# Loads cast on GpSimd's queue and transposed tile by tile, and score bursts that run across batches, in a fused attention and MLP kernel

## The chip, the cores and the metric

The kernel runs on one core of a Trainium2 chip. The metric is the device time of one execution in microseconds (us); less is better. The engines are named as in the profile: PE (TensorE matmul), PEld (its weight loads), DVE (VectorE), ACT (ScalarE), POOL (GpSimd), SP (SyncE, here only a queue that issues DMAs).

## The reference

Attention with causal mask over 8 batches and 8 heads, 576 queries, and 16 extra "beacon" keys and values that every query sees, then an MLP with a squared ReLU over the 4608 resulting tokens:

```python
k_all = np.concatenate([beacon_k, k], axis=2)      # (8, 8, 16 + 576, 64)
v_all = np.concatenate([beacon_v, v], axis=2)
scores = scale * np.matmul(q, k_all.transpose(0, 1, 3, 2))
# causal mask on the 576 keys, softmax over all 592
x = np.matmul(a, v_all)  # then laid out as (4608, 512)
h = x @ w_in             # (512, 2048)
out = (np.maximum(h, 0.0) ** 2) @ w_out            # (2048, 512)
```

Inputs and output are float32; the kernel computes in bf16 and accumulates in float32.

## The kernel before, in words

Work is cut by batch. A batch has four pairs of heads; a pair's two heads use the upper and the lower 64 rows of PE at the same time ("rows" mode). Keys come in five tiles of 128 rows (the last has 80), of which the first holds the 16 beacons.

Per batch: Q and K are brought into the transposed layout (`qT`, `kT`, head dimension on the partitions). Score matmuls (L813) write scores, transposed, into PSUM, ACT takes the exponential into `pt` (L830), DVE applies the causal mask (L848, L852), PE multiplies with V and a column of ones (AV, L869), DVE normalises into `xn` (L884, L885), and `xn` is transposed into `xT`, a ring of four batches, by SP's DMA transposes (L916; batch 0 on PE, L933). The MLP runs over nine chunks of 512 tokens: first product L997, ReLU on ACT or DVE (L1014, L1016), square on DVE (L1023), second product L1037, evacuation on ACT and a store on SP (L1062). The last chunk ends with L1080.

Score pieces. The scores of a pair are cut into four pieces with 512, 512, 512 and 128 columns for each head (`WHOLE`). A piece fills a pair of PSUM banks. PE does them in bursts, since rows mode and the full mode of the other matmuls alternate. From batch 1 on the fourth pieces of two pairs share one pair of banks (`SHARED`), with an exponential for each: 14 pieces a batch. `SIZES` gives the bursts: from batch 2 on 3, 3, 3, 3 and 2 pieces, so a batch's last burst has two.

Q, K and V. Batches 0 to 2 load Q and K strided (L635, POOL's queue, which casts to bf16 while loading; the first pair by SP and ACT, cast by copies) and transpose them on PE (L671, L674). V of batches 0 and 1 is loaded by POOL's queue with the cast in the DMA (L498, L499; `SOFT_V`). Everything else, that is V of batches 2 to 7 and Q and K of batches 3 to 7, is loaded by SP in float32 into eight staging tiles `stg` (L512, L513) and cast by POOL (L452) into `vb` or into the Q and K areas in `qk_area`. When all five tiles of Q, or of K, have been cast, one DMA transpose on SP turns 20 blocks of 128 x 128 (L543). Q and K areas, V and `qT`, `kT` are double-buffered by batch; the last Q and K tile are zeroed by POOL once (L476, L477).

Order. `Order` is a list scheduler that runs while the kernel is built: each piece of work (`Op`) has an engine, a cost, a priority, dependencies and perhaps a claim on a pool (PSUM banks, staging tiles, `pt` slots). It plays the costs forward, with a model of the DMA rings, and emits the instructions in the order that comes out. On the chip each engine follows its order and waits on semaphores. `gate` in `add_pair` holds back the scores of a pair until the MLP has come far enough. `TURNS` (L315) fixes by hand the order in which POOL issues the first loads. While PE has nothing to do near the start, `filler` emits small matmuls on an identity matrix (L571, L569; L559 first), in the window `FILL` (0.6 to 22 us of the scheduler's time); `OWED` is the number of fillers that are put in after each operation named in `ahead` whether PE has other work or not, and is 0. SP and POOL work strictly in order: an issue that waits holds all behind it.

Of the kernel before, what the change touches and what calls it, by code (L numbers as in the profile page):

```python
# [130 lines left out]
class Order:  # L131
# [5 lines left out]
    FILL = (0.6, 22.0)  # L137
    OWED = 0
# [20 lines left out]
    def run(self):  # L159
# [25 lines left out]
        now = 0.0  # L185
        mode = None
        owed = 0
        while events:
# [27 lines left out]
            while again:  # L216
                again = False
                for e in engines:
# [33 lines left out]
                    if e == "PE" and self.filler is not None and self.FILL[0] <= now < self.FILL[1] and (  # L252
                            best is None or owed):
# [50 lines left out]
        for op, e, _ in issued:  # L304
# [10 lines left out]
TURNS = ("tri0 sld0k1 sld0q1 sld0k2 sld0q2 sld0k3 sld0q3 ld0v0 ld0v1 win0 ld0v2 tri1 ld0v3 ld0v4 win1 win2 win3 bkl1 sld1k0 sld1q0 sld1k2 sld1q2 ld1v0 ld1v1 ld1v2 ld1v3 ld1v4 "  # L315
         "wout0 wout1 wout2 bkl2 sld2k0 sld2q0 wout3 sld2k2 sld2q2")
# [3 lines left out]
def kernel(  # L320
# [29 lines left out]
    def sb(name, shape, dt):  # L350
        return pool.tile(shape, dt, name=name)

    NSTG, NPT, RB = 8, 4, 4
# [9 lines left out]
    qb = [qk_area[:, (2 * i) * W:(2 * i + 1) * W].rearrange("p (g c d) -> p g c d", g=HP, c=NT)  # L363
          for i in range(2)]
    kb = [qk_area[:, (2 * i + 1) * W:(2 * i + 2) * W].rearrange("p (g c d) -> p g c d", g=HP, c=NT)
# [4 lines left out]
          for i in range(2)]  # L370
    bks = sb("bks", [128, H, D], BF16)
# [29 lines left out]
    def wait_for(later, first):  # L401
# [4 lines left out]
        pools={"ps": Banks(), "stg": Slots(NSTG), "pt": Slots(NPT)},  # L406
# [63 lines left out]
    SOFT_V = [(b, c) for b in range(2) for c in range(NT)]  # L470
# [3 lines left out]
    def add_zero(b):  # L474
        def emit(e):
            nc.gpsimd.memset(qb[b % 2][:, :, NT - 1, :], 0.0)  # L476
            nc.gpsimd.memset(kb[b % 2][:, :, NT - 1, :], 0.0)  # L477
        deps = trans[NPE - 1, "q"] + trans[NPE - 1, "k"] + trans[NPE - 2, "q"] + trans[NPE - 2, "k"]
        zero_ops[b] = add(f"zero{b}", "POOL", 1.0, emit, prio=10.0 * b - 1, deps=deps)

    def add_load(b, x, c, prio, behind=[], sync=[]):
# [6 lines left out]

        soft = (b, c) in SOFT_V
        queue = nc.gpsimd if soft else nc.sync  # L490

        if soft:

            def emit_soft(e):
                to = vb[b % 2][:, c, :, 0:D]
                insts = []
                if lo:
                    insts.append(queue.dma_start(out=to[0:Nb], in_=beacon[b].transpose([1, 0, 2])))  # L498
                insts.append(queue.dma_start(out=to[lo:rows], in_=t[b, :, t0:t0 + rows - lo, :].transpose([1, 0, 2])))  # L499
                return insts  # L500

            ld = add(f"ld{b}{x}{c}", "POOL", 1.3 if lo else 0.65, emit_soft, prio=prio, dma=0.85 * rows / 128 + 0.1 * (lo > 0), packet=0.0135,
                     behind=load_chain[-1:] + behind, sync=sync)
            load_chain.append(ld)
            cast[b, x, c] = ld
            return

        def emit_load(e):
            st = stg[ld.held[0]]
            insts = []  # L510
            if lo:
                insts.append(queue.dma_start(out=st[0:Nb], in_=beacon[b].transpose([1, 0, 2])))  # L512
            insts.append(queue.dma_start(out=st[lo:rows],  # L513
                                         in_=t[b, :, t0:t0 + rows - lo, :].transpose([1, 0, 2])))
            return insts

        ld = add(f"ld{b}{x}{c}", "SP", 1.3 if lo else 0.65, emit_load,
                 prio=prio, take=("stg", "stg", [1]), dma=1.2 * max(rows / 128, 0.72) + 0.2 * (lo > 0), behind=load_chain[-1:] + behind, sync=sync)
        load_chain.append(ld)

        def emit_cast(e):
            st = stg[ld.held[0]]
            if x == "v":
                copy_on(e, vb[b % 2][0:rows, c, :, 0:D], st[0:rows])
            else:
                dst = (qb if x == "q" else kb)[b % 2][0:rows, :, c, :]
                copy_on(e, dst, st[0:rows].rearrange("p (g u) d -> p g (u d)", u=2))

        deps = [ld]
# [7 lines left out]
        cast[b, x, c] = add(f"cast{b}{x}{c}", "POOL", 0.65, emit_cast, prio=prio, deps=deps, give=ld)  # L537

    def add_trans(b, x, prio):
        srcb, dst = (qb, qT) if x == "q" else (kb, kT)  # L540

        def emit(e):
            nc.sync.dma_start(  # L543
                out=dst[b % 2].rearrange("p g (c t) -> p (g c) t", c=NT),
                in_=srcb[b % 2].rearrange("p g c d -> p (g c d)"),
                transpose=True,
            )

        deps = [cast[b, x, c] for c in range(NT)]
        deps += [o for p in range(HP * (b - 2), HP * (b - 1)) for o in qk_ops[p]]  # L550
        trans[b, x] = [add(f"tr{b}{x}", "SP", 3.8, emit, prio=prio, deps=deps, dma=3.4, margin=2.0)]

    def filler(spot, mode, now):
# [19 lines left out]
        op = Op("fill", "PE", 0.11, emit, mode=mode)  # L573
# [180 lines left out]
    PIECES = {b: ONE_BY_ONE if b < 1 else SHARED for b in range(B)}  # L754
    SIZES = {b: [2] * 7 if b < 2 else [3, 3, 3, 3, 2] for b in range(B)}
# [29 lines left out]
    def add_scores(pairs, n, sizes, pieces):  # L785
# [10 lines left out]
        for size in sizes:  # L796
            group = work[at:at + size]
            at += size
            lead = group[0][0][0]
            prio = 100.0 * lead.p + 1000.0 * n + group[0][0][1]  # L800
            every = [part for parts in group for part in parts]
            cols = sum(t1 - t0 for _, _, _, (mms, _, _) in every for _, t0, t1, _ in mms)
            owners = list({x.p: x for x, _, _, _ in every}.values())
            box = {}

            def emit_qk(e, group=group, box=box):
                for k, parts in enumerate(group):
                    st = pair(box["qk"], k)
                    for x, _, lo, (mms, _, _) in parts:
                        for c, t0, t1, col in mms:  # L810
                            for hj in range(2):
                                hp = slice(64 * hj, 64 * hj + 64)
                                nc.tensor.matmul(  # L813
                                    st[:, hj, lo + col:lo + col + t1 - t0],
                                    kT[x.b % 2][hp, x.pr, 128 * c:128 * c + 128],
                                    qT[x.b % 2][hp, x.pr, t0:t1],
                                    start=True, stop=True,
                                )

            qk = add(f"qk{lead.p}.{n}.{group[0][0][1]}", "PE", cols / 2400.0, emit_qk, prio=prio,  # L820
                     deps=[d for x in owners for d in x.qk_deps + [x.take_pt] + early.get((x.b, x.pr, min(n, 1)), [])],
# [373 lines left out]
```

## Time and profile before

| what | value |
|---|---|
| median of 3 runs | 337.18 us (337.08 to 338.04) |
| the profiled execution | 337.61 us |
| its span | 335.7 us |
| granted PE clock, mean | 1.00 |
| DMA engines, 0 to 220 us | mean busy share mostly 0.8 and above |
| HBM read, written | 37.22 MB, 9.44 MB |

The span runs from the first to the last recorded instruction; the profiled execution's time is 1.9 us more. Times inside the trace are counted from the span's start. In rows of instructions the fields are line, engine, operation, what is written <- what is read, count, then busy time, mean duration in ns of one, and the idle time of the engine ahead of them with what ended it. In the chain in order of time a row has its start, its duration, and engine, tile, line and count. A few per cent of the matmul records are missing, so counts can be a little short.

### The profile page before, as it was taken

The numbers are of one execution on the slowest core, as the hardware profiler recorded it, in microseconds if no ns is written. First come the engines' busy times: TensorE is split into PE (matmuls) and PEld (weight loads), VectorE is DVE, ScalarE is ACT, GpSimd is POOL, SyncE is SP. The second block draws the span as 40 slices with busy tenths as digits, with TensorE's granted clock in tenths as the row PEclk, the third lists the DMA queues.
The fourth block names the chain that finished last, engine by engine and source line by source line (L and its number), as shares of the span: only waits on it lengthen the run. The fifth ranks groups of instructions, "written<-read, shape, count | busy, mean of one in ns | idle before, by whom it ended". The sixth has DMA issues, their size and how long they took to land.

```text
span 335.7 us, 7764 instructions
## 1 busy us (share of the span) xinstructions
PE 326.6 (97%) x3190; PEld 184.3 (55%) x3231; DVE 159.9 (48%) x329; ACT 194.1 (58%) x296; POOL 84.2 (25%) x130
## 2 busy tenths in 40 slices
PE   7899999999999999999999999999999999999996
PEld 5568765554555455545468945554545444444444
DVE  6689985557423762376136812681258303301400
ACT  3887977577465647574566555665576226515611
POOL 8946504513224332223242240420000000000000
PEclk9999999999999999999999999999999999999999
DMA  8999999899979996899799898973110321011003
GB/s 139 173 204 186 200 205 211 143 235 189 226 113 254 236 213 137 204 232 201 133 253 219 180 182 176 209 155 70 64 64 0 63 71 62 2 62 62 2 5 120
DMA packets 144180, 49.17 MB, mean 146 GB/s; under 512 B 130577, under 2 KB 139665, under 8 KB 144145
## 3 DMA queue, kind: packets, MB, share of 16 engines
q1 hardware_dynamic: 125168, 39.63, 58.2%
q0 software_dynamic: 18624, 8.69, 20.1%
q8 instruction: 25, 0.41, 0.5%
q10 hardware_dynamic: 352, 0.36, 0.4%
q14 instruction: 11, 0.08, 0.1%
HBM read 37.22 MB, written 9.44 MB: 139 GB/s over the span
## 4 chain that ended last, share of the span: by engine, by line
PE 91%; POOL 3%; DMA 3%; issue 1%; DVE 1%; ACT 0%; DVEq 0%
PE ps L997 37%; PE ps L1037 36%; PE ps L869 8%; PE ps L813 8%; DMA w_in<-in_moe_w_in_dram 3%; POOL vb L499 1%; PE ps L671 1%; POOL qk_area L635 1%; PE ps L1080 1%; POOL tri L435 0%; DVE g L1016 0%; POOL w_in L958 0%; DVE tri L414 0%; PE ps L933 0%; POOL vb L498 0%
## 5 line engine op out<-in xcount | busy, mean ns | idle before, releaser
L997 PE MATMUL ps<-xT,w_in 128*128 128x512 bf16 (+3 forms) x688 | 133.7, 340 | 1.2 <-DVE g L1016 0.2
L1037 PE MATMUL ps<-w_out,g 128*128 128x512 bf16 x535 | 125.1, 379 | 1.8 <-issue 0.6
L830 ACT ACTIVATE pt<-ps 128x1024 bf16<-128x1024 f32 (+3 forms) x128 | 103.1, 870 | 28.9 <-PE ps L813 27.8
L997 PEld LDWEIGHTS <-w_in 128*128 128x128 bf16 x704 | 65.5, 98 | 55.5 <-issue 4.1
L1014 ACT ACTIVATE g<-ps 128x512 bf16<-128x512 f32 (+2 forms) x111 | 63.3, 570 | 44.1 <-PE ps L997 43.9
L1037 PEld LDWEIGHTS <-g 128*128 128x128 bf16 x560 | 52.2, 98 | 61.7 <-issue 4.0
L1023 DVE TENSOR_TENSOR g<-g 128x1024 bf16<-128x1024 bf16 (+2 forms) x80 | 51.4, 648 | 65.3 <-ACT g L1014 64.8
L450 ACT COPY osb<-ps 128x512 f32<-128x512 f32 (+2 forms) x37 | 21.3, 576 | 56.7 <-PE ps L1037 43.4
L452 POOL CAST qk_area<-stg 128x512 bf16<-128x512 f32 (+2 forms) x50 | 32.7, 659 | 66.1 <-DMA stg<-in_k_dram 33.2
L848 DVE TENSOR_TENSOR pt<-pt,tri 128x1024 bf16<-128x1024 bf16 (+1 forms) x36 | 23.6, 656 | 40.7 <-ACT pt L830 40.7
L869 PEld LDWEIGHTS <-pt 128*128 128x128 bf16 (+1 forms) x960 | 33.7, 97 | 6.6 <-issue 0.6
L452 POOL CAST vb<-stg 128x512 bf16<-128x512 f32 (+1 forms) x30 | 21.9, 734 | 58.9 <-DMA stg<-in_v_dram 52.9
L1016 DVE TENSOR_SCALAR g<-ps 128x512 bf16<-128x512 f32 (+2 forms) x49 | 28.9, 590 | 15.6 <-PE ps L997 15.3
L869 PE MATMUL ps<-vb,pt 128*128 128x65 bf16 (+1 forms) x960 | 35.0, 193 | 0.3 <-DMA vb<-in_v_dram 0.3
L813 PE MATMUL ps<-qT,kT 64*128 64x80 bf16 (+6 forms) x680 | 32.1, 230 | 0.0
L885 DVE TENSOR_TENSOR xn<-ps,rcp 128x640 bf16<-128x640 f32 (+2 forms) x36 | 27.0, 751 | 1.4
L813 PEld LDWEIGHTS <-kT 64*128 64x128 bf16 x680 | 18.2, 95 | 16.3 <-issue 13.5
L884 DVE RECIPROCAL rcp<-ps 128x10 f32<-128x10 f32 (+2 forms) x36 | 7.6, 211 | 32.6 <-PE ps L869 31.5
L450 ACT COPY qT<-ps 128x576 bf16<-128x576 bf16 (+2 forms) x13 | 7.7, 601 | 4.6 <-PE ps L671 3.3
L452 DVE COPY kT<-ps 128x576 bf16<-128x576 bf16 (+2 forms) x13 | 9.0, 706 | 2.6 <-PE ps L671 2.0
L852 DVE TENSOR_TENSOR pt<-pt,tri 80x160 bf16<-80x160 bf16 x32 | 9.8, 308 | 0.0
L499 POOL DMA_DIRECT2D vb<-in_v_dram x10 | 8.5, 851 | 3.5 <-DMA w_in<-in_moe_w_in_dram 3.1
(54 smaller groups left out, 80.8 us busy)
## 6 DMA issues: line engine op xcount, KB each, us to landing
out_dram<-osb SPq DMA_DIRECT2D x17, 512.0 KB, 3.4
stg<-in_q_dram SPq DMA_DIRECT2D x20, 256.0 KB, 4.8
stg<-in_v_dram SPq DMA_DIRECT2D x18, 256.0 KB, 4.7
stg<-in_k_dram SPq DMA_DIRECT2D x15, 256.0 KB, 4.8
w_in<-in_moe_w_in_dram POOLq DMA_DIRECT2D x4, 512.0 KB, 9.6
w_out<-in_moe_w_out_dram POOLq DMA_DIRECT2D x4, 512.0 KB, 9.8
stg<-in_v_dram SPq DMA_DIRECT2D x6, 224.0 KB, 4.5
qk_area<-in_k_dram POOLq DMA_DIRECT2D x4, 288.0 KB, 12.0
```

The source lines that it names most:

```text
L450: nc.scalar.copy(dst, src)
L452: eng[e].tensor_copy(dst, src)
L813: nc.tensor.matmul(st[:, hj, lo + col:lo + col + t1 - t0], kT[x.b % 2][hp, x.pr, 128 * c:128 * c + 128], qT[x.b % 2][hp, x.pr, t0:t1], sta ...
L830: nc.scalar.activation(pt[x.take_pt.held[0]][:, :, off:off + width], pair(box["qk"], k)[:, :, lo:lo + width], AF.Exp, bias=0.0, scale=scale)
L848: nc.vector.tensor_tensor(out=d, in0=d, in1=tri[:, m0:m0 + m, :][:, None].to_broadcast([128, 2, m, 128]), op=ALU.min)
L869: nc.tensor.matmul(a[:, hj, (t - tl[0]) * (D + 1):(t - tl[0] + 1) * (D + 1)], P[0:rr, hj, o:o + 128], vb[b % 2][0:rr, c, h, 0:D + 1], star ...
L885: nc.vector.tensor_tensor(out=xn[b % 2].rearrange("p t (h d) -> p h t d", d=D)[:, 2 * pr:2 * pr + 2, tl[0]:tl[0] + nt], in0=a[:, :, :, 0:D ...
L997: nc.tensor.matmul(h[:, lo - spans[0][0]:hi - spans[0][0]], w_in_sb[:, mc, ft * 128:(ft + 1) * 128], xT[:, mc, lo % RING:lo % RING + hi - lo],
L1014: nc.scalar.activation(dst, h, AF.Relu, bias=0.0, scale=1.0)
L1016: nc.vector.tensor_scalar(out=dst, in0=h, scalar1=0.0, scalar2=None, op0=ALU.max)
L1023: nc.vector.tensor_tensor(out=d, in0=d, in1=d, op=ALU.mult)
L1037: nc.tensor.matmul(o, G[:, fc, ts * 128:(ts + 1) * 128], w_out_sb[:, fc, :], start=(fc == 0), stop=(fc == NFT - 1))
```

## The change

1. **Loads.** All tiles of V, and Q and K of batches 3 to 7, are loaded on POOL's queue with the cast in the DMA, straight into `vb` and the Q and K areas. Staging is only kept for one small tile; POOL's casts are gone. The areas are laid out tile by tile. The first load of each of batches 4 to 7 waits for the transposes of K tile 3 of the batch before.
2. **Transposes.** Q and K of batches 3 to 7 are transposed one tile (four blocks) at a time on SP, 10 DMAs a batch in place of 2. A tile's K blocks of the four pairs go to `kT` side by side; a function `keys_of` that names this order is new, while the score matmuls address `kT` by pair and tile, as before.
3. **Pieces.** In batches 3 to 7 (`FLOW = 3`) the fourth pieces of all four pairs form one piece with one exponential into a tile `rest` (in the free tail of `qk_area`), from which AV reads these keys. A batch has 13 pieces. They go into bursts of three that are filled across the batch boundary: a batch's pieces left over start a burst with the first pieces of the next.
4. **Start.** `tri0` (two mask tiles on POOL) comes behind the six strided loads, not ahead of them. No filler between 5.0 and 6.2 us of the scheduler's time; the scheduler counts 0.13 for a filler (0.11 before), and `OWED` is 1. V of batch 2 follows its Q and K in the order fixed by hand.

In the instruction streams: SP has 107 instructions (160 before), of them 50 transposes of Q and K (10 before) and none of the 91 staging loads; POOL has 91 load issues more and 80 casts less; PE has the same matmuls for scores, AV and MLP, in 49 stretches of score matmuls (52 before), and 60 filler matmuls on the identity (76 before); ACT has 15 exponentials less.

```diff
-    FILL = (0.6, 22.0)
-    OWED = 0
+    FILL = ((0.6, 5.0), (6.2, 22.0))
+    OWED = 1
...
-TURNS = ("tri0 sld0k1 sld0q1 sld0k2 sld0q2 sld0k3 sld0q3 ld0v0 ...
+TURNS = ("sld0k1 sld0q1 sld0k2 sld0q2 sld0k3 sld0q3 tri0 ld0v0 ...
...
-    NSTG, NPT, RB = 8, 4, 4
+    NSTG, NPT, RB = 1, 4, 4
...
+    rest = [qk_area[:, 4 * W + 1024 * i:4 * W + 1024 * (i + 1)].rearrange("p (h w) -> p h w", h=2) for i in range(2)]
...
+        def emit_load(e):
+            if x == "v":
+                to = vb[b % 2][:, c, :, 0:D]
+            else:
+                to = (qb if x == "q" else kb)[b % 2][:, c].rearrange("p g (u d) -> p (g u) d", u=2)
+            insts = []
+            if lo:
+                insts.append(nc.gpsimd.dma_start(out=to[0:lo], in_=beacon[b].transpose([1, 0, 2])))
+            insts.append(nc.gpsimd.dma_start(out=to[lo:rows], in_=t[b, :, t0:t0 + rows - lo, :].transpose([1, 0, 2])))
+            return insts
...
+        for c in range(NT):
+            def emit(e, c=c):
+                if x == "q":
+                    to = qT[b % 2][:, :, 128 * c:128 * c + 128]
+                else:
+                    to = kT[b % 2].rearrange("p g t -> p (g t)")[:, 128 * HP * c:128 * HP * (c + 1)].rearrange(
+                        "p (g t) -> p g t", g=HP)
+                return [nc.sync.dma_start(out=to, in_=(qb if x == "q" else kb)[b % 2][:, c].rearrange("p g d -> p (g d)"),
+                                          transpose=True)]
...
-            if b == 2 and n == 0:
-                sync = [w_ops["out", 3]]
+            if b > NPE and n == 0:
+                sync = [trans[b - 1, "k"][3]]
...
+    def add_flow(pairs, last):
...
+        pieces = WHOLE[0].pieces
+        (c, t0, t1, _), = pieces[3][0]
+        flow.append([(x, 3, 128 * n, ([(c, t0, t1, 0)], None, 128)) for n, x in enumerate(pairs)])
+        flow.extend([(x, i, 0, pieces[i])] for x in pairs for i in range(3))
+        done = []
+        while len(flow) >= 3 or (last and flow):
+            group = [flow.pop(0) for _ in range(min(3, len(flow)))]
+            add_burst(group, 0, flow_exps)
...
+                        if x is not None and (c, t) == (0, 3):
+                            keys = rest[x.take_rest.held[0]][:, hj, 128 * pr:128 * pr + 128]
```

More of the change, by code (lines that the diff above doesn't have):

```diff
@@ L405 @@
     order = Order(
[L406 removed]
+        pools={"ps": Banks(), "stg": Slots(NSTG), "pt": Slots(NPT), "rest": Slots(2)},
         limits={"late": 4, "strip": 6, "av": 4, "mlp": 4, "tp": 6},
@@ L487, in add_load @@
             t0, rows = t_start(c), rows_of(c)
[L489 to L529, printed above, removed]
+        deps = []
         if x == "v" and b >= 2:
@@ L796, in add_scores @@
         for size in sizes:
-            group = work[at:at + size]
+            add_burst(work[at:at + size], n, exps)
             at += size
[L799 to L818, printed above, removed]
```

156 lines of the change are left out of this document (103 added, 53 removed).

## The prediction

> **What bounds the kernel now.** I read three views first: busy time by engine with the chain that ended last (the page), then busy time in stretches of 10 us, then the waits of PE.
>
> ```profile
> PE 326.6 (97%) x3190; PEld 184.3 (55%) x3231; DVE 159.9 (48%) x329; ACT 194.1 (58%) x296; POOL 84.2 (25%) x130
> ...
> PE 91%; POOL 3%; DMA 3%; issue 1%; DVE 1%; ACT 0%; DVEq 0%
> ```
>
> ```profile
> 0.00:10.00 10.00, 7.67 (x115) 5.18 (x115) 6.38 (x28) 4.29 (x6) 8.52 (x18) 1.00 0.90 146
> 10.00:20.00 10.00, 9.40 (x170) 6.51 (x164) 7.03 (x24) 8.05 (x13) 8.07 (x14) 1.00 1.70 182
> 20.00:30.00 10.00, 9.86 (x156) 7.80 (x153) 9.25 (x28) 7.79 (x13) 4.63 (x6) 1.00 1.29 203
> 30.00:40.00 10.00, 9.93 (x143) 7.92 (x141) 9.26 (x24) 9.47 (x20) 6.60 (x10) 1.00 1.71 186
> ```
>
> ```profile
> PE ps L1037 <- issue: 0.6, 4, 0.2
> PE ps L997 <- DVE g L1016: 0.2, 1, 0.2
> ```
>
> The columns of the stretches are PE, PEld, DVE, ACT, POOL, granted clock, DMA share, GB/s. From 20 us on PE is busy 9.86 and more of ten; the two wait rows (total, times, longest) are all that PE waited from 24 us to the end, 0.8 us. So the loads, casts, transposes and exponentials of batches 3 to 7 are hidden today: making them cheaper is worth nothing by itself, and making them late costs one for one. Only two things can shorten the run: fewer microseconds of matmul stream, and less lost time before 20 us. Granted clock is 1.00 in each of these rows.
>
> **Part 1: bursts of score matmuls (batches 3 to 7).** The cost of entering and leaving a burst is read from the chain in order of time, at a place with nothing missing around it.
>
> ```profile
> 231.60 0.77 PE ps L813 x20
> 232.38 4.21 PE ps L1037 x19
> 236.63 1.03 PE ps L1037 x4
> 237.66 0.67 PE ps L813 x20
> 238.33 1.83 PE ps L1037 x8
> 240.16 0.91 PE ps L869 x30
> 241.13 1.67 PE ps L1037 x7
> ...
> 263.45 1.08 PE ps L1037 x5
> ...
> 277.26 8.85 PE ps L997 x41
> ```
>
> By the code 64 matmuls of 512 columns run from 263.45 to 277.26 (a few records are missing): 13.81 / 64 = 0.216 us each. The eight at 238.33 should take 1.73 and took 1.83: leaving a burst costs 0.10 us. After AV matmuls (240.16) the next eight take from 241.07 to 242.80, 1.73: those switches are free. Inside a burst two heads run side by side. The one at 237.66 streams 1280 columns by the code, 1280 x 0.216 / 512 = 0.54, and took 0.67; the one at 231.60 streams 1536, 0.65, and took 0.77. Entering costs 0.13. So one burst costs 0.23 us beyond its columns.
>
> Before, a batch has 14 pieces in bursts of 3, 3, 3, 3, 2: 5 x 5 = 25 bursts. After, a batch has 13 pieces (four fourth pieces in one) and the 65 pieces run on: 22 bursts. Columns, AV matmuls and MLP matmuls stay as many as they were. The term is 3 x 0.23 = **-0.7 us**. ACT loses 15 small exponentials, which nothing waits for.
>
> **Part 2: the start.** What stands first on POOL, PE and the DMA engines:
>
> ```profile
> 1.68 0.53 POOL L435 TENSOR_SCALAR_AFFINE_SELECT tri<-tri 128x128 bf16<-128x128 bf16 x2 [1.16 <-DVE tri L414]
> 2.17 0.76 POOL L635 DMA_DIRECT2D qk_area<-in_k_dram  x1
> ...
> 6.84 1.73 POOL L499 DMA_DIRECT2D vb<-in_v_dram  x2
> ```
>
> ```profile
> 4.89 2.03 PE L571 MATMUL ps<-ident 128*128 128x128 bf16 x30
> 6.76 0.42 PE L671 MATMUL ps<-ident,sparek 96*128 96x96 bf16 x6
> ...
> 9.66 0.45 PE L674 MATMUL ps<-ident,qk_area 96*64 96x96 bf16 x12 [0.39 <-DMA qk_area<-in_q_dram]
> ...
> 13.57 0.46 PE L869 MATMUL ps<-vb,pt 128*128 128x65 bf16 x10 [0.33 <-DMA vb<-in_v_dram]
> ...
> 17.55 0.57 PE L997 MATMUL ps<-xT,w_in 128*128 128x240 bf16 x4
> ```
>
> ```profile
> 5.19 0.83 ACT L450 CAST spareq<-g 96x768 bf16<-96x768 f32 x1 [2.43 <-DMA g<-in_q_dram]
> ```
>
> ```profile
> 2.00:3.00 1.00, 1.00 (x3) 0.36 (x4) 0.81 (x8) 0.76 (x2) 1.00 (x3) 1.00 0.79 169
> 3.00:4.00 1.00, 1.00 (x3) 0.30 (x2) 1.00 (x8) 0.00 (x0) 0.99 (x3) 1.00 1.08 354
> ```
>
> tri0 stands in front of POOL's first load and waits for VectorE until 1.68; it ends at about 2.2. With tri0 behind the six loads, the first of them can go 1.2 us earlier (2.17 against some 1.0), and all that follows tri0 (V, W_in) by the wait alone, about 0.65 us. The 30 fillers end at 6.9 although the second operand of the first transpose was cast by 6.02: with 12 of them PE is free at 5.7, so the first transpose can go about 0.65 us earlier. In all the stream has 16 fillers less, 16 x 2.03 / 30 = 1.1 us.
>
> Bounds of this term: at best -1.2 us, everything moved up by what POOL gains. At worst it is +0.3 us: the DMA engines already have a share of 0.79 and 1.08 from 2 to 4 us, so POOL's earlier loads only share them with the first K and Q, whose casts then come later; the waits at 9.66 and 13.57 then stay where they are, fillers turn into waiting, and the bit more work that VectorE has before the first MLP matmul (a Q evacuation moves to it) costs a few tenths. I take the middle of the rows that speak for it, **-0.6 us** (the 0.65 that both the fillers and the V and W_in loads give), since PE has 0.39 + 0.33 us of waits and those fillers to lose before 17.55 and hardly anything afterwards.
>
> The second new thing, one owed filler after each of 16 named operations, is inside the count of 16 fewer.
>
> The Trainium skill (TensorE: Matmul & The Clock Gate, What's actually happening) says that PE falls to half its clock after an idle window of some 3.4 us. The gap without fillers, 5.0 to 6.2, is shorter, so by that page too it costs nothing; no run here shows it yet.
>
> **Part 3: loads and transposes, hidden if they are in time.**
>
> ```profile
> L452 POOL CAST qk_area<-stg 128x512 bf16<-128x512 f32 (+2 forms) x50 | 32.7, 659 | 66.1 <-DMA stg<-in_k_dram 33.2
> L452 POOL CAST vb<-stg 128x512 bf16<-128x512 f32 (+1 forms) x30 | 21.9, 734 | 58.9 <-DMA stg<-in_v_dram 52.9
> L499 POOL DMA_DIRECT2D vb<-in_v_dram x10 | 8.5, 851 | 3.5 <-DMA w_in<-in_moe_w_in_dram 3.1
> ...
> xT<-xn SPq DMA_TRANSPOSE x35, 2.5
> ```
>
> ```profile
> 90.92 8.40 SPq L916 DMA_TRANSPOSE xT<-xn  x5
> ...
> 127.30 6.91 SPq L916 DMA_TRANSPOSE xT<-xn  x5
> ...
> 147.03 0.53 SPq L1062 DMA_DIRECT2D out_dram<-osb  x1
> ```
>
> ```profile
> 116.97 0.54 PE ps L813 x8
> ...
> 137.51 0.86 PE ps L997 x4
> ```
>
> POOL loses 80 casts (54.6 us) and gains 91 load issues of at most 0.85 us (77 us), spread over some 170 us: it stays under half busy, but now the first load of each of batches 4 to 7 waits for K transposes of the batch before (a new wait), and behind it on POOL stand all later loads. SP loses 91 issues and has 50 transposes of four blocks, which I price by xT, the same shape: 1.4 to 1.7 us each on SP (6.91 / 5, 8.40 / 5), 2.5 to landing.
>
> The tightest place is batch 4, since the burst with the last piece of batch 3 now also holds the first two of batch 4 and needs all its transposes. In the new order as much PE work stands ahead of this burst as was done in the old run about 1 us after the burst at 116.97, so it wants them at about 117 (with 1 us gained by then). On SP they stand behind the five xT transposes of batch 2, which begin no later than at 90.92: 90.9 + 5 x 1.4 + eight transposes x 1.4 + two stores x 0.53 + 2.5 = 112.7; at 1.7 each it is 116.6. Slack 0.4 to 4 us. XT of batch 3 now stands behind five Q transposes of batch 5; begun at the old 127.30, its third tile lands at 127.3 + 3 x 1.4 + 2.5 = 134, and the first MLP matmuls of the chunk that reads it stood at 137.51, about 136 in the new order. Batches 5 and 7, also spanned by a burst, come out looser in the same way. So I price this part at 0, and if the cover goes, each late microsecond is one on the path.
>
> What stands against this part by rows is VectorE beside POOL:
>
> ```profile
> L499 POOL DMA_DIRECT2D vb<-in_v_dram x4: 737/884/893, 26.3 to 29.4; - x4
> ```
>
> ```profile
> L452 DVE COPY qk_area<-qk_area x12: 344/348/357, 30.5 to 55.7; 96x768 bf16<-96x768 bf16 x12
> ```
>
> With VectorE 92% busy (20 to 30 us) a V load's issue took 0.74 to 0.89 us, as the 0.85 of all ten, so I use that. The Trainium skill (SBUF — State Buffer, SBUF: two separate sides) says that GpSimd cannot write descriptors while VectorE runs in a two-port mode, as some copies do, so that a load issued there starves. The rows bear it out only weakly, and the copies inside SBUF, the second row, end at 56 us, before the loads of batches 3 to 7.
>
> **Sum.** -0.7 - 0.6 + 0 = -1.3 us. The profiled execution took 337.61 (span 335.7), 0.43 above the median of 337.18; the terms are differences, so I take them from the median: 337.18 - 1.3 = **335.9 us**.
>
> **Rivals.** (a) The start gives all it can: -0.7 - 1.2 = 335.3. For it: everything before 17.55 hangs on POOL's queue. Against: DMA share over 1. (b) The start gives nothing, since DMA, or VectorE at 9.25 and ACT at 9.47 of 10 in the stretch from 20 to 40, hold PE instead, and PE only waits where it filled: -0.7 + 0.3 = 336.8, no change. This is also the case in which the change does not do at the start what it says. (c) Slower: POOL's loads stretch. Place: POOL, batches 5 to 7, where loads wait for the transposes of the batch before, and the transposes of SP hold back xT. From the last K transposes of batch 4 (about 111) to those of batch 5 (xT at 127.3, ten transposes and a store further, 144) the loop takes some 33 us, a batch of PE work 36 (127.30 - 90.92). At 0.85 us an issue that fits; from about 1.5 us on, 11 loads x 0.65 = 7 us later, the Q transposes push xT of batches 3, 4 and 5 past their MLP chunk, each by 7 us less 2 to 4 of slack, of which the next batch finds part made up already; I take 4 in all after the gains: 335.9 + 4 = 340. For it: a loop through two queues that did not exist; against: POOL's rows. The Trainium skill's page named in part 3 would bring about this case, by the same price.
>
> **How the numbers follow.** Forecast 335.9 (own range 335.5 to 336.4) 0.45; (a) 0.18; (b) 0.19; (c) 0.18. A measurement of this kernel tells about 0.3%, 1.0 us, from no change; the line is at 336.17. Faster: most of the forecast's case (0.33) and (a), 0.51. Within: the rest of the forecast's case and (b), 0.31. Slower: (c), 0.18. The range takes in (a), (b) and the mild end of (c): 335.0 to 338.5.
>
> **What would show it.** Part 1: 22 bursts of L813 from batch 3 on, 20 or 24 matmuls each, with the same 0.13 and 0.10 around them. Part 2: the first load on POOL near 1.0 us, the first transposes on PE near 6.1, the first MLP matmul near 17.0. Part 3: PE idle in batches 3 to 7 as low as now, no wait of PE or PEld on a DMA into qT, kT, xT or vb. The prediction is wrong if such waits add up to over 1 us, if the first K and Q land over half a microsecond later than now, or if POOL's load issues go above 1.2 us.

## The result, and the profile after

| | median | runs |
|---|---|---|
| before | 337.36 us | 337.08 to 338.04, 6 runs |
| after | 349.47 us | 345.68 to 354.06, 6 runs |

The ratio is 1.032 (95% interval 1.029 to 1.035): the change made the kernel 3% slower, where 335.9 us had been forecast and 338.5 was the top of the range. The profiled execution took 349.13 us, its span is 347.2 (335.7 before). The medians are of all six runs; the two slowest of after (350.98 and 354.06 us), over 1.5% above its fastest, are left out of the ratio.

The page of the kernel after, busy time and the chain that ended last:

```profile
PE 328.8 (95%) x3174; PEld 185.7 (53%) x3215; DVE 154.7 (45%) x327; ACT 193.6 (56%) x283; POOL 102.9 (30%) x141
...
PE 79%; DMA 13%; POOL 2%; SPq 2%; issue 2%; DVE 1%; ACT 0%; POOLq 0%
```

PE is idle for 347.2 - 328.8 = 18.4 us, 9.1 before: 9.3 of the 11.5 us that the span grew by. In the chain DMA has 13% for 3%; 4% of the span is `xT`, the other DMA pieces are loads of the first 45 us. The rest of the 11.5 us is 2.2 us more of busy PE, although it now has less to do. The waits of PE say on what:

```profile
PE ps L1033 <- DMA xT<-xn: 6.6, 2, 3.4
...
PE ps L1033 <- ACT pt L836: 1.3, 1, 1.3
PE ps L905 <- DMA vb<-in_v_dram: 1.1, 1, 1.1
...
PE ps L586 <- DMA bks<-in_beacon_k_dram: 0.8, 2, 0.5
```

L1033 is the first MLP product (L997 before). It waits twice for `xT`, and a third time, from 109.76 to 111.07, by the row for an exponential that had ended 0.46 us before PE went on. The fourth `xT` transpose of batch 2, which by the code this chunk needs, was issued at 102.3 and landed 8.7 us later, at about 111.0 (landing is counted from the start of the issue on SP). So all three are `xT`, of batches 1, 2 and 3: 7.9 of the 9.3 us. The waits on `vb` (0.3 before) and `bks` make up the remainder. The longest of the three, of batch 3, in the timelines of DVE and SP and in the chain in order of time:

```profile
131.57 0.82 DVE L921 TENSOR_TENSOR xn<-ps,rcp 128x640 bf16<-128x640 f32 x1
```

```profile
130.25 7.24 SPq L531 DMA_TRANSPOSE qT<-qk_area  x5
137.61 7.04 SPq L952 DMA_TRANSPOSE xT<-xn  x5
```

```profile
140.26 7.32 DMA xT<-xn
...
147.71 1.86 PE ps L1033 x4
```

Two things are late here. DVE had normalised the last heads of batch 3 by 132.39, but SP was issuing five Q transposes of batch 5 and began with `xT` 5.2 us later, at 137.61. The third of the `xT` transposes, which the chunk needs by the code, went out at 140.26 and then took 7.32 us to landing, where the median before was 2.5. PE had nothing else to do from 144.29 on. By these numbers either delay alone would have been hidden: issued at once, the third would have landed at about 142.4, and with 2.5 us to landing at 142.8.

Batch 2 is the same case: normalised by 95.35, begun at 98.05 behind Q and K transposes, its fourth transpose in at 111.0 for a need at 109.76; without the hold it would have been in at 108.3, with 2.5 us to landing at 104.8. In batch 1 the landing did it alone: normalised by 59.56, begun at 59.59, the fourth transpose issued at 64.1 and in after 7.7 us; with 2.5 it would have been in at 66.6, and PE wanted it from 68.77 on.

What POOL does just ahead of batch 3's transposes, in its timeline:

```profile
124.90 0.83 POOL L513 DMA_DIRECT2D qk_area<-in_k_dram  x1
125.72 3.52 POOL L513 DMA_DIRECT2D qk_area<-in_q_dram  x4
...
136.00 1.76 POOL L513 DMA_DIRECT2D vb<-in_v_dram  x2 [0.48 <-DMA qk_area<-in_q_dram]
137.98 0.73 POOL L513 DMA_DIRECT2D vb<-in_v_dram  x1 [0.22 <-issue]
```

The loads of a whole batch went out in 14 us, 0.73 to 0.91 us each, right ahead of the transposes. The DMA issues (count, median us to landing) show how long everything that is transposed now takes:

```profile
xT<-xn SPq DMA_TRANSPOSE x35, 6.8
...
qT<-qk_area SPq DMA_TRANSPOSE x25, 6.9
kT<-qk_area SPq DMA_TRANSPOSE x25, 4.6
```

`xT` had 2.5 before. Last, the stretches around two of the waits (columns as in the prediction), one of them of 1 us:

```profile
60.00:70.00 10.00, 8.61 (x98) 4.44 (x98) 1.89 (x4) 6.42 (x9) 7.95 (x10) 1.00 2.12 119
70.00:80.00 10.00, 7.86 (x71) 4.04 (x73) 3.54 (x7) 4.65 (x6) 3.37 (x4) 0.83 1.53 215
...
73.00:74.00 1.00, 1.00 (x19) 0.74 (x20) 0.00 (x0) 0.75 (x2) 0.74 (x2) 0.50 1.31 279
...
140.00:150.00 10.00, 6.58 (x42) 2.80 (x41) 0.84 (x2) 4.32 (x6) 0.00 (x0) 0.88 1.56 186
150.00:160.00 10.00, 9.79 (x86) 5.00 (x86) 4.88 (x9) 5.98 (x10) 5.75 (x8) 0.95 1.23 149
```

The granted clock fell to 0.83, 0.88 and 0.95; in stretches of 1 us it was 0.50 for some 3.4 us after each of the two long waits, and 1.00 after the one of 1.31. Had PE worked through these thirty microseconds, that would be 1.7 + 1.2 + 0.5 = 3.4 us of its work: the busy time that was added although fillers and bursts became fewer.

### The profile page after: what moved, and what is told of

Its sections match the earlier page's. It is cut to its first block, busy times and chain, and to the rows that moved or that the text cites. A ratio compares the mean times of both kernels' runs of the same rounds, so it can differ in the third digit from the quotient of the medians.

```text
span 347.2 us, 7641 instructions
## 1 busy us (share of the span) xinstructions
PE 328.8 (95%) x3174; PEld 185.7 (53%) x3215; DVE 154.7 (45%) x327; ACT 193.6 (56%) x283; POOL 102.9 (30%) x141
## 4 chain that ended last, share of the span: by engine, by line
PE 79%; DMA 13%; POOL 2%; SPq 2%; issue 2%; DVE 1%; ACT 0%; POOLq 0%
PE ps L1033 34%; PE ps L1073 31%; PE ps L905 7%; PE ps L809 6%; DMA xT<-xn 4%; DMA qk_area<-in_k_dram 3%; DMA bks<-in_beacon_k_dram 3%; DMA w_in<-in_moe_w_in_dram 2%; SPq L952 2%; POOL qk_area L619 1%; PE ps L1116 1%; PE ps L655 1%; POOL vb L513 0%; DVE xn L921 0%; ACT pt L836 0%
## 5 line engine op out<-in xcount | busy, mean ns | idle before, releaser
L1033 PE MATMUL ps<-xT,w_in 128*128 128x512 bf16 (+3 forms) x690 | 134.1, 342 | 9.0 <-DMA xT<-xn 6.6
L836 ACT ACTIVATE pt<-ps 128x1024 bf16<-128x1024 f32 (+4 forms) x108 | 97.2, 959 | 6.2 <-PE ps L809 4.5
L1033 PEld LDWEIGHTS <-w_in 128*128 128x128 bf16 x704 | 65.7, 98 | 63.7 <-issue 13.9
L1050 ACT ACTIVATE g<-ps 128x512 bf16<-128x512 f32 (+2 forms) x116 | 65.2, 564 | 51.4 <-PE ps L1033 50.0
L1059 DVE TENSOR_TENSOR g<-g 128x1024 bf16<-128x1024 bf16 (+2 forms) x80 | 50.5, 635 | 62.5 <-ACT g L1050 61.6
L881 DVE TENSOR_TENSOR pt<-pt,tri 128x1024 bf16<-128x1024 bf16 (+1 forms) x36 | 22.6, 627 | 42.1 <-ACT pt L836 42.1
L1052 DVE TENSOR_SCALAR g<-ps 128x512 bf16<-128x512 f32 (+2 forms) x44 | 26.8, 610 | 28.8 <-PE ps L1033 28.4
L513 POOL DMA_DIRECT2D vb<-in_v_dram x40 | 33.8, 854 | 15.5 <-DMA w_in<-in_moe_w_in_dram 4.1
L809 PEld LDWEIGHTS <-kT 64*128 64x128 bf16 x680 | 19.2, 96 | 16.6 <-issue 12.8
L513 POOL DMA_DIRECT2D qk_area<-in_k_dram x25 | 21.4, 874 | 0.1
L513 POOL DMA_DIRECT2D qk_area<-in_q_dram x25 | 21.3, 862 | 0.0
L512 POOL DMA_DIRECT2D qk_area<-in_beacon_k_dram x5 | 2.7, 535 | 59.2 <-issue 45.5
L512 POOL DMA_DIRECT2D vb<-in_beacon_v_dram x8 | 4.4, 550 | 24.1 <-PE ps L905 20.0
```

Source lines behind the costliest of these rows:

```text
L513: insts.append(nc.gpsimd.dma_start(out=to[lo:rows], in_=t[b, :, t0:t0 + rows - lo, :].transpose([1, 0, 2])))
L809: nc.tensor.matmul(st[:, hj, lo + col:lo + col + t1 - t0], kT[x.b % 2][hp, x.pr, 128 * c:128 * c + 128], qT[x.b % 2][hp, x.pr, t0:t1], sta ...
L836: nc.scalar.activation(pt[x.take_pt.held[0]][:, :, off:off + width], pair(box["qk"], k)[:, :, lo:lo + width], AF.Exp, bias=0.0, scale=scale)
L881: nc.vector.tensor_tensor(out=d, in0=d, in1=tri[:, m0:m0 + m, :][:, None].to_broadcast([128, 2, m, 128]), op=ALU.min)
L1033: nc.tensor.matmul(h[:, lo - spans[0][0]:hi - spans[0][0]], w_in_sb[:, mc, ft * 128:(ft + 1) * 128], xT[:, mc, lo % RING:lo % RING + hi - lo],
L1050: nc.scalar.activation(dst, h, AF.Relu, bias=0.0, scale=1.0)
```

## The experiments

Each run gave its time beside runs of the kernel before on the same chip (337.4 to 337.6 us median in each group). The theory after reading the trace: a transpose on SP lands late while loads of GpSimd's queue are under way, and `xT` has too little slack for it. What SP's order adds to it was not part of this theory; it is read from the timelines of the same runs.

**Loads and transposes alone.** The kernel after, with start, pieces and bursts taken back.

```diff
-    FILL = ((0.6, 5.0), (6.2, 22.0))
-    OWED = 1
+    FILL = ((0.6, 22.0),)
+    OWED = 0
...
-TURNS = ("sld0k1 sld0q1 sld0k2 sld0q2 sld0k3 sld0q3 tri0 ld0v0 ...
+TURNS = ("tri0 sld0k1 sld0q1 sld0k2 sld0q2 sld0k3 sld0q3 ld0v0 ...
...
-    FLOW = 3
+    FLOW = 8
```

> The changed kernel with its loads on GpSimd's queue and its tile-by-tile transposes, but the score pieces, bursts, fillers and the place of tri0 as before. Theory (two queues): the small DMA transposes of xT share the DMA engines with a backlog of GpSimd's loads and land after 6 to 8 us instead of 2.5, so PE waits for xT: 346 to 352 us here too, xT landing 6 us or more (median). Rival (spanning bursts): PE is late because bursts wait for the transposes of the next batch: at most 340 us here, no wait of PE for xT.

348.88 us, ratio 1.034 (1.030 to 1.039). All of the loss is still there, so it is not in the bursts that run on, nor in the start. `xT` lands after 5.9 us in the median. Its waits of PE:

```profile
PE ps L1033 <- DMA xT<-xn: 8.3, 2, 7.2
```

The long one has both parts again: `xT` of batch 3 was normalised by 126.60, and SP, behind Q and K transposes, began with it at 134.69.

**Staging back on SP, tiles still transposed one by one.**

```diff
+        ld = add(f"ld{b}{x}{c}", "SP", 1.3 if lo else 0.65, emit_load, ...
...
+        cast[b, x, c] = add(f"cast{b}{x}{c}", "POOL", 0.65, emit_cast, prio=prio, deps=deps, give=ld)
```

> The changed kernel, but all loads that were on SP before are there again, staged in float32 and cast by POOL; transposes tile by tile, the joint pieces, the bursts and the start are kept. Theory (two queues): xT lands in 2.4 to 4 us and the time is 335.5 to 338.5. Rival (SP itself, 50 small transposes in front of xT): xT lands in 6 us or more and the time stays at 345 or above. Rival (spanning bursts): xT lands early but PE waits before L809 and the time is over 341.

354.95 us, ratio 1.050 (1.045 to 1.054): the slowest of all. The landing came out as the theory said (`xT` 2.5 us, `qT` 3.3, `kT` 2.5), the time did not. The timeline of SP shows why; there is no gap in it:

```profile
139.73 1.68 SPq L556 DMA_TRANSPOSE kT<-qk_area  x1
141.51 1.21 SPq L556 DMA_TRANSPOSE qT<-qk_area  x1
142.82 7.14 SPq L977 DMA_TRANSPOSE xT<-xn  x5
150.06 0.53 SPq L1123 DMA_DIRECT2D out_dram<-osb  x1
```

A transpose of four blocks holds SP for 1.2 to 1.7 us. Fifty of them, 35 of `xT`, and the staging loads: SP's own queue is then on the chain that ended last, with 8.2% (L556), 5.7% (loads) and 4.7% (`xT`) of the span; the chain of the kernel before has no SP in it. PE waits 5.3 us on `kT` and 3.3 on `xT`. So transposing by tile has a price of its own, and only the loads' move to GpSimd made room for it on SP. A wait ahead of the scores is also what the rival of the spanning bursts expected; the run before, with the bursts as they were, speaks against it for the whole change, and this run does not separate the two.

**Loads held behind xT.**

```diff
-            if b > NPE and n == 0:
-                sync = [trans[b - 1, "k"][3]]
+            if b >= NPE and n == 0:
+                sync = [xt_ops[b - 2, NT - 1]] + ([trans[b - 1, "k"][3]] if b > NPE else [])
```

> The changed kernel, in which the first load of batches 3 to 7 also waits until xT of the batch two before has landed. Theory (two queues): xT lands in about 2.5 to 3.5 us, the waits of PE for xT go, 337 to 342 us (a load that starts later may cost up to 3). Rival (SP itself): xT lands in 6 us or more still, 347 to 351.

346.04 us, ratio 1.027 (1.023 to 1.030). This is above the 337 to 342 expected. `xT` is back at 2.5 us, SP issues it as soon as it is normalised (batch 3 at 132.69, after 132.66), and no wait for it is left: the run takes both delays away together. But the loads, later now, have the transposes of Q and K (8.2 and 7.9 us to landing) in their midst, and the wait moved there:

```profile
PE ps L809 <- DMA kT<-qk_area: 5.5, 5, 2.0
```

**The transposes by themselves, beside loads of different queues.** Two small kernels without the reference's work. The first:

> Not the reference's computation: in ten phases, five DMA transposes of four blocks on SP beside three loads of 24 tiles' rows (256 B each in memory, 786 KB a load): none, GpSimd with cast, GpSimd without cast, ACT's queue without cast, GpSimd with cast of rows of 2 KB; each twice. Theory (two queues): transposes land in 2.4 to 3 us alone and in 5 us or more beside GpSimd's casting loads; if it is the number of packets, GpSimd without cast is as bad and rows of 2 KB are mild. Rival (SP itself): 2.4 to 3 us in all phases.

Alone 2.4 to 2.5 us. Beside GpSimd's casting loads 5.6 to 8.1, without the cast 6 to 15, with rows of 2 KB still 6 to 9: neither the cast nor short rows are the reason. Its stage with ACT's loads is inconclusive: the delay ran on ACT behind its own load issues, so the transposes went out from 67.8 on, when the loads were nearly in (the last at 70.4). The second gives the delay to DVE:

> Measures the disputed cost by itself: it leaves out the reference's computation altogether. Eight stages, each twice, have SP issue transposes of 128 rows: five of four blocks, in stages with nothing beside them, beside four 768 KB loads issued by ACT without a cast, beside the same loads issued by GpSimd with a cast all at once, one after the other's landing, and two at a time, behind the same loads on SP's own queue, and at last one transpose of twenty blocks alone and beside GpSimd's casting loads. Theory (a backlog on GpSimd's queue delays the transposes): 2.4 to 2.6 us to landing alone, at most 3.5 beside ACT's loads and behind SP's own, 6 to 8 beside GpSimd's whole backlog, and less, 3.5 to 6, with one load at a time. Rival (any load's traffic delays a transpose, as bytes are shared): 5 to 8 beside ACT's and SP's loads as well. Rival (GpSimd's writing of descriptors delays them, not the backlog): one load at a time as bad as all at once, and short again as soon as the last issue is over. The one of twenty blocks: by a delay for each transpose some 8 to 9 us instead of 4; by a delay for each block 15 or more.

The landing (min/median/max) in eight stages of the first of two rounds, in this order: five transposes alone; beside ACT's loads; beside GpSimd's casting loads all at once; one at a time; two at a time; behind loads on SP's own queue (with SP's row); then twenty blocks alone, and beside GpSimd's loads.

```profile
DMA to landing us min/median/max: 2.5/2.5/2.6
...
DMA to landing us min/median/max: 5.6/7.4/7.9
...
DMA to landing us min/median/max: 6.2/6.9/7.5
...
DMA to landing us min/median/max: 2.5/3.1/5.6
...
DMA to landing us min/median/max: 4.3/5.1/6.7
...
L79 SPq DMA_TRANSPOSE turned<-src x5: 1257/1265/4184, 120.3 to 128.4; - x5
DMA to landing us min/median/max: 2.5/2.5/6.6
...
DMA to landing us min/median/max: 4.9/4.9/4.9
...
DMA to landing us min/median/max: 11.8/11.8/11.8
```

My theory was too narrow: ACT's loads, without a cast, delay as much as GpSimd's (7.4 against 6.9; 6.5 against 6.9 in the second round). What counts beside loads of another queue is how much of them is under way: 3.1, 5.1, 6.9 us with one, two, four at a time (3.9, 5.3, 6.9 in the second round). Behind loads on SP's own queue the median is 2.5, but the transposes are not earlier for it:

```profile
110.21 9.95 SPq L70 DMA_DIRECT2D loadf<-in_v_dram  x4
120.26 9.42 SPq L79 DMA_TRANSPOSE turned<-src  x5
```

SP issued the loads until 120.16. The first transpose then landed after 6.6 us, right behind the last load (126.4), the second was held for 4.18 us on SP, and the others went out from 125.8 on, with the loads about done. Counted from when their source was ready (112.53), the five were in after 14.4 to 18.5 us, against 6.3 to 11.7 beside GpSimd's loads all at once. On one queue the wait stands ahead of the issue, and a transpose is quick only where the order on SP puts it ahead of the loads. The kernel before has that order: its five `xT` transposes go out one after another with no load between them (6.91 us in batch 3), and land after 2.5 us there, 3.6 in batch 2 (medians). The Trainium skill (DMA: Bandwidth & Descriptors, Queues, rings and completion order) says that a DMA engine takes turns between the queues that have work for it, a packet at a time; the times with one, two and four loads agree in their direction, and no row here shows the packets themselves.

**Pieces and bursts alone, start alone, and both, on the kernel before.** The edits are points 3 and 4 of the change.

> Before with the joint pieces and the bursts that run on alone; loads, transposes and start as before. Theory (the prediction's term stands: 22 bursts for 25 and four exponentials' lead in less): 336.3 to 336.9, that is 0.4 to 1.0 below the kernel before, with the four joint exponentials' bursts at 0.77 us of PE between their neighbours. Rival (the bursts that run on delay the next batch's first products or the xT of the batch before, a cost that the loads hide in the whole change): 338 or more, with a wait of PE on xT or on an exponential over 1 us.

> Before with the change's order of the first loads (the triangle's work behind the strided loads), its pause in the filling matmuls from 5.0 to 6.2 us and their cost alone. Theory (as read in the changed kernel's trace, nothing comes earlier where it counts): 337.2 to 338.0, the first products of the MLP within 0.3 us of 17.55. Rival (the prediction's term): 336.5 to 336.9, the first products at 17.0 or before.

> Before with the joint pieces, the bursts that run on and the change's start: all of the change but the loads and the transposes. Theory (bursts -0.7, start 0 to +0.5): 336.5 to 337.3, and 11 us or more below the whole change, so that loads and transposes hold all that was lost. Rival (the parts disturb one another, as the order of the work is searched as a whole): 338 or more.

Start alone 338.76 us, ratio 1.004 (1.002 to 1.006), above the 337.2 to 338.0 expected. Both 338.31, 1.003 (1.001 to 1.005): not the 336.5 to 337.3 of the theory, but 11.2 us below the whole change, so nearly nothing of the whole loss is left without loads and transposes. Pieces alone 343.23, 1.014 (1.011 to 1.018), a miss. Its profiled execution (339.86 us) is the fastest of the six; what makes the median 3.4 us longer is not shown. Its chain shows the one long wait of PE:

```profile
172.58 0.23 DVE rcp L937
172.81 0.69 SPq L969
...
174.87 2.48 DMA xT<-xn
...
177.39 3.22 PE ps L1050 x28
```

The landing is short, but SP is late. The reciprocal that the chain names belongs to batch 5. `xT` of batch 4 had been normalised by 164.98, and in SP's timeline loads, a store and a whole Q transpose (167.34 to 172.21) stand ahead of it, so that it began at 172.30, 7.3 us later. Here no load on GpSimd's queue is to blame: SP's order alone can cost a wait, also with 2.48 us to landing. From "start" to "both" the bursts add -0.45 us in the medians, less than this measurement can tell.

**At most two loads under way.**

```diff
+            if b >= NPE:
+                sync = sync + [load_chain[-2]]
             add_load(b, x, c, lp + 0.1 * n, behind, sync)
```

> The changed kernel, but each load of batches 3 to 7 waits on GpSimd's queue until the load two before it has landed, so that at most two are under way. Theory (transposes are late because of how many bytes of another queue's loads lie ahead of them; with two 768 KB loads at a time they landed after 5.1 to 5.3 us instead of 6.9): xT to landing falls from 6.8 to about 4 us, PE's waits on xT from 6.6 to under 3 us, the time to 339 to 344. Rival (the pace makes the loads themselves late, and the wait moves to kT, qT or vb): 345 or more with waits of PE on those over 4 us. Rival (transposes of tiles hold SP's queue, not the traffic): xT's landing falls but the time stays at 347 to 350.

345.12 us, ratio 1.026 (1.021 to 1.030). `xT` lands after 3.6 us and no wait for it is left, as forecast (it is also issued as soon as it is normalised, batch 3 at 132.84 after 132.81); the time is the rival's. Its profiled execution (343.06 us, the fastest of the four) shows `kT` late instead:

```profile
PE ps L809 <- DMA kT<-qk_area: 2.4, 2, 1.6
```

With the 1.2 us on `vb`, at the start, that is 3.6, under the 4 us of the rival, so the median is not fully accounted for.

**Loads on GpSimd, Q and K transposed whole.**

```diff
+            return [nc.sync.dma_start(
+                out=dst[b % 2].rearrange("p g (c t) -> p (g c) t", c=NT),
+                in_=srcb[b % 2].rearrange("p c g d -> p (c g d)"), transpose=True)]
```

> The changed kernel with its loads on GpSimd's queue, but Q and K of a batch each turned by one transpose of twenty blocks on SP, as before; the products read queries and keys in the order in which these write them. Theory (the loads' traffic delays whatever is turned beside it): xT still 5 us or more to landing in the median, qT and kT 8 to 12 us, PE's waits on xT, qT and kT together over 5 us, 344 to 350. Rival (the fifty transposes of tiles, 1.2 to 1.3 us of SP each, are what holds the rest back): xT at 3 us or less, 336 to 340. If both count, 340 to 344.

344.69 us, ratio 1.022 (1.017 to 1.027). (Lines not shown cut Q at the same rows as K, and let the first load of the next batch wait for the whole K transpose.) Some 40% of the loss goes away with the small transposes; the rest stays. `xT` still takes 5.8 us to landing, but for batches 2 and 3 SP now issues it as soon as it is normalised (batch 3 at 133.18, after 133.15), and their waits are gone. What stays is the wait of batch 1, where the landing alone was the cause:

```profile
PE ps L1043 <- DMA xT<-xn: 2.7, 1, 2.7
PE ps L596 <- DMA bks<-in_beacon_k_dram: 2.5, 2, 1.6
```

The second row is a load at the start of the run, so part of what is left in this kernel is not from the transposes. The 2.7 us on `xT` are under the 5 expected, and `qT` and `kT` land after 6.8 us, not 8 to 12.

**V alone on GpSimd's queue**, on the kernel before.

```diff
-    SOFT_V = [(b, c) for b in range(2) for c in range(NT)]
+    SOFT_V = [(b, c) for b in range(B) for c in range(NT)]
```

> Before with V of batches 2 to 7 loaded by GpSimd's queue with a cast, as batches 0 and 1 are; Q and K staged by SP and turned whole as before. That is 36 loads off SP and 30 casts off GpSimd, and a third of the staged bytes on the other queue. Theory (bytes of another queue beside transposes are what costs): xT's landing 2.5 us in the median but 4 to 6 where V's five loads run beside it, PE's waits on xT 0 to 2 us, 337 to 340. Rival (SP's queue is what is short, any load off it helps): 334.5 to 336.5. Rival (V's landing itself comes late for the AV products): waits of PE on vb over 1 us, 338 or more.

Two further lines, not shown, keep Q and K staged by SP and hold each V load until the AV products of the batch two before are done. 345.29 us, ratio 1.023 (1.022 to 1.025). PE waits 3.0 us on `vb`, as the third expectation had it, but at the start and for another reason: the wait for W_out, which holds SP's first load back, had gone to GpSimd with V, so SP brought Q and K of batch 3 from 1.74 us on, in the midst of the first loads, and the first MLP matmul came at 24.81. With the wait given back to SP:

```diff
-            if b == 2 and n == 0:
+            if (b == 2 or b == NPE) and n == 0:
                 sync = [w_ops["out", 3]]
```

> The kernel before with V of batches 2 to 7 loaded by GpSimd's queue with a cast, like the run with V on GpSimd, but with the first load of batch 3 held on SP until the fourth part of W_out has landed, so that Q and K of batch 3 no longer share the start. In the run without that hold 7.3 us were lost before 36 us of the span, and 0.1 us behind it. Theory (the loss there was the start's, and a third of the bytes on the other queue costs little): 336.8 to 338.3, the first products of the MLP within 0.5 us of 17.55, xT's landing 2.5 to 3.5 us in the median. Rival (V's loads beside the transposes cost too, only hidden there): 339 or more with PE waits on xT, kT or qT over 1 us. Rival (loads off SP's queue help): 335 to 336.5.

337.59 us, ratio 1.001 (1.000 to 1.002): no loss, and no gain. Its DMA issues:

```profile
xT<-xn SPq DMA_TRANSPOSE x35, 3.5
...
qT<-qk_area SPq DMA_TRANSPOSE x5, 9.0
kT<-qk_area SPq DMA_TRANSPOSE x5, 8.5
```

Here too the transposes land 1 to 3 us later than before, but PE waits for none of them. These 36 of the 91 loads on the other queue still fit into the slack; all of them do not (344.69 with whole transposes). And 36 loads and 30 casts less on SP and GpSimd gain nothing, as nothing waited for them.

**Both remedies together**, with pieces, bursts and start as before.

> The changed kernel's loads on GpSimd's queue with at most two under way, Q and K turned whole by SP, and pieces, bursts and start as before: the two remedies together, and nothing else of the change. Theory (the loss is the transposes' lateness beside unpaced loads plus SP's time for fifty small transposes, both undone here): xT at 4 us or less to landing, PE's waits on xT, qT and kT together under 2 us, 336.5 to 340. Rival (loads on another queue than SP's cost in themselves, as nothing then orders them against the transposes): 341 or more, with xT, kT or qT waits over 2 us.

350.08 us, ratio 1.037 (1.034 to 1.040): a clear miss. A whole transpose waits until all of its paced loads have landed, and so starts late (SP waits 69.2 us for loads of Q and 22.4 for loads of K, most of it hidden from PE):

```profile
PE ps L819 <- DMA kT<-qk_area: 8.9, 3, 3.6
```

Paced loads want transposes by tile (the run with both has 345), and whole transposes want loads that come quickly. No version tried beats the kernel before.

## Why the prediction was wrong

**Part 1, bursts, right in size as far as it can be seen.** The chain of after has the bursts at 0.77 and 0.78 us, for 20 and for 24 matmuls:

```profile
207.94 0.77 PE ps L809 x20
...
212.27 0.78 PE ps L809 x24
```

That is the cost forecast, and by the code there are 22 of them. The 0.7 us were not seen on their own: -0.45 between two kernels, under what the measurement tells.

**Part 2, the start: -0.6 expected, about +0.5 found.** The first transposes on PE came at 6.17 (6.76 before), as the text said, and the first load went out at 1.36 (2.17), 0.8 us earlier where 1.2 was forecast. What failed is the step from there: "all that follows tri0 (V, W_in) by the wait alone, about 0.65 us". In POOL's timeline of after:

```profile
5.72 0.76 POOL L436 TENSOR_SCALAR_AFFINE_SELECT tri<-tri 128x128 bf16<-128x128 bf16 x2
6.43 0.54 POOL L512 DMA_DIRECT2D vb<-in_beacon_v_dram  x1
6.96 1.71 POOL L513 DMA_DIRECT2D vb<-in_v_dram  x2
```

`tri0` now takes 0.76 us instead of 0.53 and stands ahead of V, so V went out at 6.96 for 6.84 and PE stood before AV for it:

```profile
13.20 0.28 PE L905 MATMUL ps<-vb,pt 128*128 128x65 bf16 x4 [1.07 <-DMA vb<-in_v_dram]
...
18.05 0.57 PE L1033 MATMUL ps<-xT,w_in 128*128 128x240 bf16 x4
```

Most of the lead was waited away there: AV went on at 13.20, for 13.57 before. From there to the first MLP matmul the changed kernel takes 4.85 us for 3.98, so that this matmul came at 18.05 for 17.55. In that stretch PE has 24 fillers for 12, the owed ones among them; whether they are what costs the time no run shows. Rival (b) had this outcome, with +0.3. The run of the start alone agrees: 18.02, and 1.15 us over before in the medians.

**Part 3, the step that decided: the price of 0.** It rests on two terms that failed. The first are transposes "which I price by xT, the same shape: [...] 2.5 to landing". That row was right for a kernel whose loads and transposes stand in one order on SP's queue, and was carried to one where the loads are on another queue; landing became 6.8. The second is `xT` of batch 3, "begun at the old 127.30": the text lets it stand "behind five Q transposes of batch 5" and charges nothing for them. They held SP until 137.49, and `xT` began 5.2 us after it was normalised (124.84 and 127.30 before: 2.5 us). The sum "127.3 + 3 x 1.4 + 2.5 = 134" against a need at 136 had 2 us of slack, 3.4 when landing is counted from the start of the issue, as the views do. Measured, the third transpose landed at 147.58 for a need at 144.29: 3.3 us late, a wait of 3.42. The `xT` of batches 1 and 2, where the other two waits stand, are in no sum of the text, and for batch 1 the landing alone made the wait. SP's time per transpose held (medians 1.23 to 1.29 us). The lower clock behind the long waits then came on top, up to 3.4 us. The sentence "each late microsecond is one on the path" was right; the start and the landing that went into it were those of another situation.

**Rival (c)** had the side, the victim and part of the path: Q transposes on SP did push `xT` of batch 3 past its MLP chunk, together with the long landing. Its condition did not hold: POOL's issues stayed at 0.73 to 0.95 us, and VectorE did not hold them up. Its 340 us was too little, and the waits came at batches 1 to 3, not 3 to 5. The page cited for it (the Trainium skill, SBUF — State Buffer) is neither borne out nor refuted by POOL's rows of this kernel.

**What stays open.** For each of the three waits the trace says which delay made it. How the whole loss divides between landing and SP's time is known only through kernels in which the order changes too: the 4.4 to 4.8 us that whole transposes or pacing give back each do not add up (350 with both). Whether some order by hand could hide all loads on GpSimd's queue was not tried. Making transposes on ACT's queue, apart from SP, was not tried either.

## What to carry to other kernels

The same four-block transpose took 2.5 us to landing alone and some 7 beside loads of another queue, so its time belonged to its surroundings and not to its shape. Before taking such a duration from a trace, ask which queue's transfers ran beside it, and whether the change moves them to another queue. When loads leave the queue that also carries transposes, their order against each other is lost; compute the slack of each transpose anew, with what it takes beside a backlog and with what stands ahead of it on its own queue (here 5.2 us), and find the one with the least slack first. Check a cause that the chain names against the engine's timeline: twice here it named a reciprocal of the next batch where the transpose had stood behind others on SP. Work that nothing waits for, like casts and staging loads here, is worth nothing when removed, and its removal can bring transfers forward into the way of something tight.

## What the runs showed of the hardware that was not expected

- Transposes of four blocks: 2.5 us to landing alone, 7.4 (second round 6.5) beside four 768 KB loads of ACT's queue, 6.9 beside GpSimd's, 3.1 (3.9) beside one of GpSimd's at a time; twenty blocks 4.9 alone and 11.8 beside GpSimd's.
- A wait of PE of 3.42 us was followed by half speed: four matmuls of 512 columns in 1.86 us at 147.71, 0.47 each for 0.216. So was one of 3.15 us (clock 0.50, above), and one of 2.70 in the run with whole transposes (again 1.86 us for four, at 72.72). After a wait of 2.50 us (pieces alone, at 177.39) 28 matmuls of 256 columns took 3.22 us, 0.115 each, nearly full speed, and after one of 2.80 (both remedies, at 210.17) 20 score matmuls took 0.84 us, as elsewhere. The Trainium skill (TensorE: Matmul & The Clock Gate, What's actually happening) puts the idle window at some 3.4 us; here waits shorter than that already cost the clock, and their length alone does not decide it.
- In the second small kernel four DVE copies of 128x512 float32 took 1.81 us beside ACT's load issues and 4.53 beside GpSimd's, both times. In the kernel after itself no group of DVE work became longer (the product of L1059 690 ns, 706 before).
